# Opening of an FFT filter and max-of-two MoE kernel: another order of loads, preparations and the first stage of batch 1

## Chip, cores and metric

The kernel runs on one core of one Trainium2 chip. The metric is device time in microseconds (us), the median of the runs of one program. Engines are named as the profile names them: PE (TensorE, matmul; PEld its weight loads), DVE (VectorE), ACT (ScalarE), POOL (GpSimd) and SP (SyncE, which only issues DMAs here).

## What is computed

```python
X = np.fft.rfft(x, axis=1)                       # x: 8 x 3072 x 256
Y = X * (filt_r + 1j * filt_i)[None]             # filters: 1537 x 256
y = np.fft.irfft(Y, n=3072, axis=1)
h1, h2 = y @ w1, y @ w2                          # w1, w2: 256 x 1024
out = np.maximum(h1, h2) @ w_out                 # w_out: 1024 x 256
```

The kernel uses max(h1, h2) = relu(h1 - h2) + h2. With Wd = w1 - w2 and M = w2 @ w_out the last two lines become relu(y Wd) w_out + y M.

## The kernel before

**Stages.** Each of the 8 batches passes a first transform over 96 points (f1 for batch 1 and s1 for later ones; s1t for batch 0), a regrouping of its result into bt, six visits, each of which makes a second transform (s2, PSUM tile px), a product with the filter F (pq) and the way back (s3, tile pz), a regrouping into zr, a last transform (s4, PSUM tile py, result y), and the MoE part in tiles of 384 tokens, eight tiles per batch.

For batch 0 the two regroupings are transposes on PE: t1 fills bt[0], s3t and t2 fill zT and zr[0]. For batch 1 and later they go through DRAM: f1 or s1 write `ad` (SP), f1_read or s1_read read `ad` into bt (SP); s3 writes `zd`, z_read reads it into zr.

**The MoE loop.** A tile tt has eight steps, one for each block j of 128 hidden columns; step 8*i + j is counted within a batch. A step issues, in this order: moe_h(tt, j), two matmuls with Wd into a PSUM tile ph and a relu copy to gt on DVE or ACT; a visit of the next batch if `mid` has one for this step; three or four of the 30 matmuls of moe_o for the tile before (po: two with M and eight with Wo for each of three blocks c of 128 tokens); then what `todo` holds for the step; and at j = 4 s4 of the next tile (j = 6 at the batch's last tile). So tile 0's output matmuls run in steps 8 to 15, beside tile 1's moe_h.

**What sets the order.** Every engine runs its instructions in program order; the schedule is written out by hand. `plan(b, step, fn, ...)` puts a call in `todo` at a step, plan_f1 places f1 (c = 1 to 15) and f1_read of batch 1, plan_f2 places the visits, the loads of x of the batch after (load_xf on SP, fold on POOL), z_read and s1_read. An instruction waits by semaphore for what it reads and for the buffer that it writes. PSUM tiles of the pool `ps` come from a ring of six, those of `pso` (po) from a ring of two.

**Queues.** POOL issues load_x (x of batches 0 and 1, one call loads the xb tile of two c; x(1,0), x(1,2), x(1,4), x(1,6) below are load_x(1, c, 2)), load_f (the filters), load_wo (w_out as bf16 into Wo), the output, and it computes products of the opening, prep_wd and fold. SP issues load_w (w1, w2 into WS, the tile that w1f and w2f are views of), double_f of the second filter part, the ad, bt, zd and zr transfers and load_xf.

**The opening.** load_f(0) loads filter columns w = 0 to 7, load_f(1) w = 8 to 11, each into partitions 0 to 31 of two groups g, for real and imaginary part ri. double_f(h, g, ri, engine) copies such a quarter to the 32 partitions beside it: for h = 0 on DVE (L130), for h = 1 by DMA on SP (L132). fix_f sets one row. Visits 0 to 3 of batch 0 read the h = 0 quarters, visits 4 and 5 the h = 1 quarters. products(v) computes one half of a visit's product on DVE and, for v in 0, 2, 3, 4, the other on POOL; v = 5 shares it.

**Preparations.** cast_w2(h, c) casts a quarter of w2 to bf16 (DVE, L285), prep_t(jp) transposes four blocks of it into w2T (PE L299, ACT L300), prep_m multiplies w2T and Wo to M (16 matmuls, L306, and a copy on ACT, L308). prep_wd(h) computes half of Wd on POOL (L292). table_ct makes CT, which s1 of batch 2 reads.

The calls of the opening that the change moves, and the schedule of tile 0, stand at L580 to L640 and L677 to L688.

Of the kernel before, what the change touches and what calls it, by code (L numbers as in the profile page):

```python
# [8 lines left out]
FP32 = mybir.dt.float32  # L9
# [17 lines left out]
def kernel(  # L27
# [55 lines left out]
    def load_x(b, c, n):  # L83
        for k in range(c, c + n):
            xb[b, k] = x_tile(b, k)[0:NP]
        src = x[b].rearrange("(p m) d -> p m d", m=NM)
        m0 = 4 * (c % 2)
        G.dma_start(out=xb[b][0:NP, m0:m0 + 4 * n], in_=src[:, 4 * c:4 * c + 4 * n, :])  # L88
# [37 lines left out]
    def double_f(h, g, ri, engine):  # L126
        w0, w1 = WP[h]
        o_, i_ = F[64 * g + 32:64 * g + 64, ri, w0:w1], F[64 * g:64 * g + 32, ri, w0:w1]
        if engine is V:
            V.tensor_copy(o_, i_)  # L130
        else:
            nc.sync.dma_start(out=o_, in_=i_)  # L132
# [6 lines left out]
    def fix_f():  # L139
        V.tensor_copy(F[32:33, 0, 0, 0], FN[32:33])  # L140
# [28 lines left out]
    load_f(0)  # L169
    load_f(1)  # L170
    load_fn()
    load_x(1, 0, 2)

    def table_c():
        p96 = init.tile([128, 1], FP32)
# [111 lines left out]
    def load_wo():  # L287
        G.dma_start(out=Wo, in_=moe_w_out.rearrange("(c p) j -> p c j", p=128))

    def prep_wd(h, engine):  # L290
        js = slice(512 * h, 512 * h + 512)
        engine.tensor_tensor(Wd[:, :, js], w1f[:, :, js], w2f[:, :, js], OP.subtract)  # L292

    def prep_t(jp):
# [162 lines left out]
    def out_block(tt, c):  # L457
# [2 lines left out]
        E = G if tt < 8 * B - 2 else nc.sync  # L460
        E.dma_start(out=dst, in_=ot[tt // 2][:, 3 * (tt % 2) + c])  # L461

    def moe_o(tt, k0, k1):
        y_, g_ = yt[tt], gt[tt]
        for k in range(k0, k1):
            c, e = divmod(k, 10)
            n = (e + 2) % 10 if tt == 0 else e
            q = 3 * tt + c
            blk = slice(128 * c, 128 * c + 128)
            if e == 0 and (q % 2 == 0 or q == 24 * B - 1):  # L470
                po[0] = pso.tile([128, 2, D], FP32, tag="po", name="po")
            p_ = po[0][:, q % 2]
            if n < 2:
                TE.matmul(p_, y_[:, n, blk], M[:, n], start=(e == 0), stop=(e == 9))  # L474
            else:
                TE.matmul(p_, g_[:, n - 2, blk], Wo[:, n - 2], start=(e == 0), stop=(e == 9))  # L476
            if e == 9 and q >= 24 * B - 2:
                e = q % 6
                if q % 2 == 0:
                    S.activation(ot[tt // 2][:, e], p_, AF.Copy)  # L480
                else:
                    V.tensor_copy(ot[tt // 2][:, e], p_)
                out_block(tt, c)
            elif e == 9 and q % 2 == 1:
                if q % 6 == 1:
                    ot[tt // 2] = opool.tile([128, 6, D], FP32, tag="ot", name="ot")
                e = q % 6
                V.tensor_copy(ot[tt // 2][:, e - 1:e + 1], po[0])  # L488
                for qq in (q - 1, q):
                    out_block(qq // 3, qq % 3)  # L490

# [64 lines left out]
    def spin(n):  # L556
        for _ in range(n):
            pd = ps.tile([128, 512], FP32, tag="ps", name="pd")
            TE.matmul(pd, W1[:, 0:128], W1, start=True, stop=True)  # L559
# [12 lines left out]
    for c in range(8):  # L572
# [5 lines left out]
        if c < 7:  # L578
            spin(2)
    bt[0] = bpool.tile([128, NU, D], BF16, tag="bt", name="bt")  # L580
    for n in range(6):
        t1(n, S if n % 2 else V)
    put_v(0, 0, table_v(0, 0))
    for g in range(2):
        for ri in range(2):
            double_f(0, g, ri, V)
            if g == 0 and ri == 0:
                fix_f()
    xs = {}

    def stage_x(v):
# [6 lines left out]
    def products(v):  # L598
        pool = pq0 if v > 2 else pqpool
        pq = [product(V, v, 0, pxs[v][0], pool)]  # L600
        if v == 5:
            pq.append(shared_product(v, 1, pxs[v][1], xs[v], pool))
        else:
            pq.append(product(G, v, 1, xs[v], pool) if v in POOLED else product(V, v, 1, pxs[v][1], pool))
        return pq
# [11 lines left out]
    put_v(1, 1, table_v(1, 1))  # L617
    for v in (1, 0, 2):
        pqs[v] = products(v)
    s3t(1, pqs[1])  # L620
    pxs[4] = s2(0, 4)
    stage_x(4)
# [7 lines left out]
        pqs[v] = products(v)  # L630
    for v in (4, 5):
        s3t(v, pqs[v])
    for c in (2, 4):
        load_x(1, c, 2)
    prep_wd(0, G)
    load_wo()
    load_x(1, 6, 2)
    prep_wd(1, G)
    table_ct()
    setup.close()  # L640
    apool = ctx.enter_context(tc.tile_pool(name="apool", bufs=3))
# [4 lines left out]
    f1(1, 0, S)  # L646
    spin(1)
    t2(0, (V, S))
    spin(2)
    s4(0)  # L650
    spin(2)


# [2 lines left out]
    def plan(b, step, fn, *a):  # L656
        todo.setdefault((b + step // 64, step % 64), []).append((fn, a))
# [17 lines left out]
            plan(b, steps[-1] + (6 if b else 11), s1_read, b + 2)  # L675

    plan(0, 2, t2, 1, (V,))  # L677
    for h in range(2):
        for c in range(2):
            plan(0, 3 + 2 * h + c, cast_w2, h, c)  # L680
    plan(0, 5, prep_t, 0)
    plan(0, 7, prep_t, 1)
    plan(0, 8, prep_m)
    for c in range(2, 8):
        plan(0, 8 * (c - 2) + 8, t2, c, (V,))
    plan_f1(0, 1, (0, 1, 1, 3, 4, 4, 5, 6, 6, 7, 8, 10, 11, 11, 12), 13)
    plan_f2(0, (24, 28, 31, 35, 38, 42, 46), ((0,), (1,), (2,), (3,), (4,), (5,), (6, 7)),
            (6, 10, 14, 18, 21, 25, 29, 33), (14, 18, 21, 25, 28, 32, 36, 40))  # L688
    for b in range(1, B - 1):
        plan_f2(b, (7, 14, 18, 24, 31, 38, 42) if b > 1 else (14, 18, 24, 30, 34, 39, 42), ((0, 1), (2,), (3,), (4,), (5,), (6,), (7,)),  # L690
# [49 lines left out]
```

## Time and profile before

| | us |
|---|---|
| runs of the kernel (three) | 503.27, 505.98, 503.62; median 503.62 |
| profiled execution, whole | 503.8 |
| profiled execution, span from first to last instruction | 502.0 |
| PE busy within the span | 488.4 (97%) |
| DVE busy | 331.9 (66%) |
| ACT busy | 308.3 (61%) |
| POOL busy | 257.5 (51%) |
| mean granted TensorE clock | 0.992 of full |

The profile gives one execution. "Busy" counts instructions, not DMA issues' waiting; a matmul's busy time includes its way through the array, so that matmuls overlap: two of ph last 0.49 us together but take 0.33 us of the chain. The page cuts the span into 40 slices of 12.55 us; a digit is the busy share in tenths. In a timeline row stand the start, the time from the start to the end of the group, the engine, the line in the kernel, the operation, the output and input tiles, how many, and in brackets how long the engine was idle before and what ended that. A row of DMA issues gives the bytes of one and the time from issue to landing.

### The profile page before, as it was taken

How to read it: one execution, taken by the hardware profiler on the slowest of the kernel's cores; microseconds unless marked ns; L12 is line 12 of the kernel's file. 1: busy time of each engine (PE TensorE's matmuls, PEld its weight loads, DVE VectorE, ACT ScalarE, POOL GpSimd, SP SyncE). 2: the span in 40 equal slices, each digit the busy share in tenths (PEclk: the TensorE clock that was granted, in tenths of full speed). 3: DMA queues.
4: the chain of work that ended last, by engine and by line, in shares of the span. 5: the costliest groups of instructions: out<-in, count | busy, mean ns of one | idle time of the engine just before them, and what ended most of it. 6: DMA issues, size and time to landing. Idle time of an engine off the chain costs nothing.

```text
span 502.0 us, 13079 instructions
## 1 busy us (share of the span) xinstructions
PE 488.4 (97%) x5299; PEld 362.1 (72%) x5303; DVE 331.9 (66%) x518; ACT 308.3 (61%) x629; POOL 257.5 (51%) x338
## 2 busy tenths in 40 slices
PE   8688999999999999999999999999999999999997
PEld 3455777777777777777777777777777777777775
DVE  7876688457865777457765687557765687555553
ACT  6776478647774676557764586647774465544442
POOL 7893569547463864645654855537632221222220
PEclk9989999999999999999999999999999999999999
DMA  7999789995799667986779558896769235411112
GB/s 125 150 252 217 230 229 290 306 274 171 212 268 260 175 204 234 250 229 189 198 244 275 187 177 245 235 239 197 197 181 255 78 111 153 168 65 64 64 64 84
DMA packets 77966, 97.20 MB, mean 194 GB/s; under 512 B 8017, under 2 KB 54354, under 8 KB 77842
## 3 DMA queue, kind: packets, MB, share of 16 engines
q1 hardware_dynamic: 64642, 66.73, 49.6%
q0 software_dynamic: 13264, 29.64, 20.3%
q8 instruction: 41, 0.67, 0.6%
q14 instruction: 19, 0.16, 0.1%
HBM read 53.87 MB, written 47.19 MB: 201 GB/s over the span
## 4 chain that ended last, share of the span: by engine, by line
PE 90%; DMA 5%; POOL 2%; issue 1%; ACT 1%; DVE 0%; SPq 0%; POOLq 0%; DVEq 0%
PE po L476 34%; PE ph L448 33%; PE po L474 8%; PE pz L399 5%; PE py L428 4%; PE pa L349 2%; DMA F<-in_filt_r_dram 2%; PE px L376 2%; DMA Wo<-in_moe_w_out_dram 2%; POOL xb L88 1%; DMA F<-F 1%; PE pr L549 1%; POOL pq L382 0%; PE pt L528 0%; PE pm__1132 L306 0%
## 5 line engine op out<-in xcount | busy, mean ns | idle before, releaser
L476 PE MATMUL po<-Wo,gt 128*128 128x256 bf16 x1536 | 261.0, 273 | 0.2 <-DMA Wo<-in_moe_w_out_dram 0.2
L452 ACT ACTIVATE gt<-ph 128x384 bf16<-128x384 f32 x321 | 157.0, 496 | 147.9 <-PE ph L448 147.3
L461 POOL DMA_DIRECT2D out_dram<-ot x186 | 102.6, 555 | 187.1 <-DVE ot L488 184.4
L476 PEld LDWEIGHTS <-gt 128*128 128x128 bf16 x1536 | 146.6, 98 | 66.1 <-issue 10.3
L450 DVE TENSOR_SCALAR gt<-ph 128x384 bf16<-128x384 f32 x191 | 104.9, 552 | 63.1 <-PE ph L448 59.9
L382 DVE TENSOR_TENSOR pq<-px,F 128x1024 bf16<-128x1024 f32 x91 | 107.0, 1219 | 24.2 <-PE px L376 22.6
L448 PEld LDWEIGHTS <-Wd 128*128 128x128 bf16 x1024 | 96.5, 98 | 12.9 <-POOL Wd L292 1.4
L103 POOL TENSOR_TENSOR xb<-XF 128x512 bf16<-128x512 f32 x48 | 61.2, 1276 | 41.3 <-DMA XF<-in_x_dram 21.2
L488 DVE COPY ot<-po 128x512 f32<-128x512 f32 x95 | 65.1, 685 | 25.3 <-PE po L476 25.0
L104 POOL TENSOR_TENSOR xb<-XF 128x512 bf16<-128x512 f32 x48 | 61.0, 1271 | 0.0
L403 ACT ACTIVATE zt<-pz 128x512 bf16<-128x512 f32 x84 | 45.6, 595 | 11.5 <-PE pz L399 8.4
L353 ACT ACTIVATE at<-pa 128x512 bf16<-128x512 f32 x96 | 51.8, 610 | 1.2 <-PE pa L349 0.8
L428 PE MATMUL py<-G,zr 96*128 96x96 bf16 x512 | 32.7, 206 | 0.2
L428 PEld LDWEIGHTS <-zr 96*128 96x128 bf16 x512 | 29.0, 97 | 2.5 <-DVE zr L552 0.4
L399 PE MATMUL pz<-pq,VP 64*64 64x256 bf16 x336 | 21.9, 281 | 0.0
L376 PE MATMUL px<-bt,U 64*64 64x256 bf16 x384 | 19.8, 278 | 1.2 <-ACT VQ L273 0.7
L399 PE MATMUL pz<-pq,VQ 64*64 64x256 bf16 x336 | 20.9, 269 | 0.0
L349 PE MATMUL pa<-xb,CT 64*64 64x512 bf16 x192 | 19.5, 383 | 0.0
L399 PEld LDWEIGHTS <-VP 64*64 64x64 bf16 x336 | 9.7, 105 | 13.3 <-issue 13.3
L376 PEld LDWEIGHTS <-U 64*64 64x64 bf16 x384 | 10.4, 109 | 3.9 <-issue 3.3
L559 PE MATMUL pd<-W 128*128 128x512 bf16 x30 | 10.5, 462 | 1.7 <-DVE zero L145 1.5
L552 DVE COPY zr<-pr 96x1024 bf16<-96x1024 bf16 (+1 forms) x8 | 5.2, 649 | 8.0 <-PE pr L549 8.0
(429 smaller groups left out, 609.7 us busy)
## 6 DMA issues: line engine op xcount, KB each, us to landing
out_dram<-ot POOLq DMA_DIRECT2D x186, 128.0 KB, 3.3
XF<-in_x_dram SPq DMA_DIRECT2D x96, 192.0 KB, 4.6
ad<-at SPq DMA_DIRECT2D x56, 192.0 KB, 3.3
bt<-ad SPq DMA_DIRECT2D x14, 768.0 KB, 9.1
zd<-zt SPq DMA_DIRECT2D x42, 256.0 KB, 2.7
zr<-zd SPq DMA_DIRECT2D x56, 192.0 KB, 4.8
WS<-in_moe_w_dram SPq DMA_DIRECT2D x4, 512.0 KB, 5.1
xb<-in_x_dram POOLq DMA_DIRECT2D x8, 192.0 KB, 5.8
```

What stands on the lines that cost most here:

```text
L103: G.tensor_tensor(t_[:, 0], f[:, 0], f[:, 1], OP.add)
L104: G.tensor_tensor(t_[:, 1], f[:, 0], f[:, 1], OP.subtract)
L353: S.activation(at[:, m0:m0 + 2], pa[g], AF.Copy)
L382: E.tensor_tensor(pq, px.rearrange("p (o i) d -> p o i d", o=1).to_broadcast([128, 2, 2, D]), F[:, :, 2 * v:2 * v + 2, s], OP.mult)
L399: TE.matmul(pz[g][64 * s:64 * s + 64, i], tab[64 * g:64 * g + 64, 2 * v + i, s], pq[s][64 * g:64 * g + 64, q, i], start=(q == 0), stop=(q ...
L428: TE.matmul(py[:, m], zr[b][:, 4 * i + m, 128 * dc:128 * dc + 128], G1, start=True, stop=True)
L448: TE.matmul(ph, Wd[:, dc, 128 * j:128 * j + 128], y_[:, dc], start=(dc == 0), stop=(dc == 1))
L450: V.tensor_scalar(gt[tt][:, j], ph, 0.0, None, OP.max)
L452: S.activation(gt[tt][:, j], ph, AF.Relu)
L461: E.dma_start(out=dst, in_=ot[tt // 2][:, 3 * (tt % 2) + c])
L476: TE.matmul(p_, g_[:, n - 2, blk], Wo[:, n - 2], start=(e == 0), stop=(e == 9))
L488: V.tensor_copy(ot[tt // 2][:, e - 1:e + 1], po[0])
```

## The change

- x(1,0) is no longer issued by POOL ahead of the products, but between products(0) and products(2).
- Of the four h = 0 filter copies on DVE, the first (g = 0, real) stands ahead of the bt copies of t1. fix_f and the other three stay behind put_v(0, 0, ...), fix_f now ahead of the three.
- prep_wd computes a quarter (256 columns) at a time. POOL's order behind the products was x(1,2), x(1,4), Wd half 0, Wo, x(1,6), Wd half 1; it is x(1,2), Wo, Wd quarters 0 and 1, x(1,4), quarters 2 and 3, x(1,6).
- The two casts of w2's first half stand in the opening, on both sides of s4(0); those of the second half come in steps 3 and 4 (were 5 and 6). prep_t(0) comes in step 3 (was 5), prep_m in step 9 (was 8).
- FIRST gives the order of tile 0's output matmuls: the Wo matmuls of blocks c = 0 and 2, then their M matmuls, then block c = 1. Since blocks 0 and 2 lie in two po tiles, po is kept by q // 2 % 2.
- f1 of batch 1, c = 1 to 15, comes in steps 0, 1, 1, 4, 5, 5, 6, 8, 9, ... 15 instead of 0, 1, 1, 3, 4, 4, 5, 6, 6, 7, 8, 10, 11, 11, 12; f1_read in step 16 (was 13). The visits of batch 1, its z_read and s1_read of batch 2 come two steps later. load_xf and fold of batch 2 stay where they were: load_xf(2, 2), in step 14, is thus now ahead of the last ad write and of f1_read on SP.

```diff
-    load_x(1, 0, 2)
...
     def prep_wd(h, engine):
-        js = slice(512 * h, 512 * h + 512)
+        js = slice(256 * h, 256 * h + 256)
...
+    FIRST = ([(c, e) for c in (0, 2) for e in range(8)] + [(c, e) for c in (0, 2) for e in (8, 9)]
+             + [(1, e) for e in range(10)])
...
-            c, e = divmod(k, 10)
-            n = (e + 2) % 10 if tt == 0 else e
+            c, e = divmod(k, 10) if tt else FIRST[k]
+            n = e if tt else (e + 2) % 10
...
-                po[0] = pso.tile([128, 2, D], FP32, tag="po", name="po")
-            p_ = po[0][:, q % 2]
+                po[q // 2 % 2] = pso.tile([128, 2, D], FP32, tag="po", name="po")
+            p_ = po[q // 2 % 2][:, q % 2]
...
-                V.tensor_copy(ot[tt // 2][:, e - 1:e + 1], po[0])
+                V.tensor_copy(ot[tt // 2][:, e - 1:e + 1], po[q // 2 % 2])
...
+    double_f(0, 0, 0, V)
     for n in range(6):
         t1(n, S if n % 2 else V)
     put_v(0, 0, table_v(0, 0))
-    for g in range(2):
-        for ri in range(2):
-            double_f(0, g, ri, V)
-            if g == 0 and ri == 0:
-                fix_f()
+    fix_f()
+    double_f(0, 0, 1, V)
+    for ri in range(2):
+        double_f(0, 1, ri, V)
...
     for v in (1, 0, 2):
         pqs[v] = products(v)
+        if v == 0:
+            load_x(1, 0, 2)
...
-    for c in (2, 4):
-        load_x(1, c, 2)
+    load_x(1, 2, 2)
+    load_wo()
     prep_wd(0, G)
-    load_wo()
+    prep_wd(1, G)
+    load_x(1, 4, 2)
+    prep_wd(2, G)
+    prep_wd(3, G)
     load_x(1, 6, 2)
-    prep_wd(1, G)
...
     t2(0, (V, S))
+    cast_w2(0, 0)
     spin(2)
     s4(0)
+    cast_w2(0, 1)
...
-    for h in range(2):
-        for c in range(2):
-            plan(0, 3 + 2 * h + c, cast_w2, h, c)
-    plan(0, 5, prep_t, 0)
+    for c in range(2):
+        plan(0, 3 + c, cast_w2, 1, c)
+    plan(0, 3, prep_t, 0)
     plan(0, 7, prep_t, 1)
-    plan(0, 8, prep_m)
+    plan(0, 9, prep_m)
...
-    plan_f1(0, 1, (0, 1, 1, 3, 4, 4, 5, 6, 6, 7, 8, 10, 11, 11, 12), 13)
-    plan_f2(0, (24, 28, 31, 35, 38, 42, 46), ((0,), (1,), (2,), (3,), (4,), (5,), (6, 7)),
+    plan_f1(0, 1, (0, 1, 1, 4, 5, 5, 6, 8, 9, 10, 11, 12, 13, 14, 15), 16)
+    plan_f2(0, (26, 30, 33, 37, 40, 44, 48), ((0,), (1,), (2,), (3,), (4,), (5,), (6, 7)),
             (6, 10, 14, 18, 21, 25, 29, 33), (14, 18, 21, 25, 28, 32, 36, 40))
```

## The prediction

> **What bounds the kernel now.** I read the page's slices first. PE is full from the fourth slice on, at the full granted clock; only the first 50 us of the 502.0 us span hold idle time of PE.
>
> ```profile
> PE   8688999999999999999999999999999999999997
> PEclk9989999999999999999999999999999999999999
> ```
>
> So the end moves only by PE work added or removed, and by PE idle time in the first 50 us or newly made later. The change adds no matmul. Next the PE timeline from 34 us shows where PE idles while tile 0 runs: for the second half of Wd, for a cast of w2, and shortly for Wo.
>
> ```profile
> 37.48 0.62 PE L448 MATMUL ph<-y__984,Wd 128*128 128x384 bf16 x2 [0.19 <-ACT y__984 L432]
> ...
> 41.07 0.50 PE L448 MATMUL ph<-y__984,Wd 128*128 128x384 bf16 x2 [0.67 <-POOL Wd L292]
> ...
> 45.35 0.56 PE L299 MATMUL pt<-I,w2b 128*128 128x128 bf16 x7 [0.70 <-DVE w2b L285]
> ...
> 46.64 0.60 PE L476 MATMUL po<-Wo,gt 128*128 128x256 bf16 x4 [0.18 <-DMA Wo<-in_moe_w_out_dram]
> ```
>
> From first ph (37.48) to first po (46.64) are 9.16 us. Their work at the chain's prices (ph pair 0.33, f1 0.22, eight transposes 0.45, py 0.34): nine ph pairs, ten f1, t2(1), s4(1), two prep_t = 6.86. So 2.3 us are idle. From 46.64 on the chain of waits is PE behind PE, apart from small gaps: 455.36 us to the end.
>
> The POOL timeline shows the order of its loads; the third row is Wo, the fourth x(1,6).
>
> ```profile
> 33.83 1.06 POOL L88 DMA_DIRECT2D xb<-in_x_dram  x2
> 34.90 2.36 POOL L292 TENSOR_TENSOR Wd<-WS 128x1024 bf16<-128x1024 f32 x1
> 37.19 0.93 POOL L288 DMA_DIRECT2D Wo<-in_moe_w_out_dram  x1
> 38.12 0.52 POOL L88 DMA_DIRECT2D xb<-in_x_dram  x1
> 38.65 2.36 POOL L292 TENSOR_TENSOR Wd<-WS 128x1024 bf16<-128x1024 f32 x1
> ```
>
> The DMA view, asked for single issues, gives landings (last column, us after the issue): Wo 9.4, so 46.6; x(1,6), queued behind Wo, 10.9, so 49.0; x(1,2), issued 33.83 with no Wo ahead, 5.3, so 39.1.
>
> ```profile
> Wo<-in_moe_w_out_dram POOLq DMA_DIRECT2D x1, 512.0 KB, 9.4
> xb<-in_x_dram POOLq DMA_DIRECT2D x1, 384.0 KB, 10.9
> xb<-in_x_dram POOLq DMA_DIRECT2D x1, 384.0 KB, 5.3
> ```
>
> POOL's transfers are thus served one after another: Wo held x(1,6) until 2.4 us after its own landing. Last, batch 1's first visit. SP's timeline and the waits of 60 to 64 us: bt is read at 56.88, lands 5.8 us later at 62.7, and px wants it at 62.97. There is no slack.
>
> ```profile
> 56.88 1.22 SPq L338 DMA_DIRECT2D bt<-ad  x2
> PEld L376 <- DMA bt<-ad: 0.3, 1, 0.3
> ```
>
> **Opening.** DVE now copies bt at 15.64, 16.54 and 17.43, then the four filter quarters from 18.15 to 23.32 (1.22 each, fix_f 0.28). The first quarter's last load (8 KB, issued 8.66, 7.0 to land) arrives at 15.7, so the moved copy runs 15.8 to 17.0, bt follows back to back to 19.05, and the last quarter ends at 22.9: 0.4 us earlier. bt 0.9 us later is hidden: px of visit 0 waits for ACT's last bt (18.94) anyway.
>
> But products 4 and 5 wait for the second filter half: its last load is issued by POOL at 22.28, its doubling on SP at 26.45 lands 4.0 later at 30.45, and DVE and POOL start product 4 at 30.60 and 30.63. While a filter copy runs on DVE, POOL's issues take 1.25, 1.49, 1.24 and 1.17 us, else 0.48 to 0.58; each ends just behind a copy. So the first copy, moved to 15.8, holds POOL's issue of 15.66 until 17.0, 0.8 us; POOL later escapes one copy. The last load is issued 0 to 0.5 us earlier.
>
> [...]
>
> x(1,0) is issued behind POOL's first product: about 25.7 instead of 23.43. Product 0 starts at 23.5 instead of 24.02, and the 0.52 of issue goes behind it, so product 3 still ends at about 30.4: nothing won on POOL. Its data now meets the last doubling, not the third. The third, which met it, took 5.4; the second, which didn't, 3.2; the last 4.0. Opening: from -0.3 (earlier issue) to +1.4 (4.0 becoming 5.4). I take 0: the earlier issue against a partial collision, since the doubling goes out beside x(1,0), not after it.
>
> **Tile 0.** POOL ends product 5 at 33.89. Then x(1,2) 0.53, Wo 0.93, two quarters of Wd 1.18 each (half of 2.36), x(1,4) 0.53, two quarters, x(1,6): Wo issued 34.4 instead of 37.19; Wd quarters ready at 36.5, 37.7, 39.4, 40.6; x(1,4) issued 37.7 instead of 34.36; x(1,6) 40.6 instead of 38.12. If each cast of w2 (0.41) blocks POOL as the filter copies did, the last quarter comes at 42.2, just when ph of j=6 wants it; I take nothing, at most 0.4.
>
> Two casts go into DVE's idle gaps before y (0.97) and the first at (0.63): free; without those gaps 0.82. Three f1 leave steps 0 to 7. DVE, which now runs unbroken from 38.36 to 45.89, then needs from 41.09 only cast, gt, cast, y, at, 0.41+0.54+0.41+0.54+0.68, until 43.7. That frees the PSUM room (six in the ring) of tile 1's first ph, so PE is ready for po at 44.1.
>
> Wo: it lands 5.5 to 6.2 us behind the x ahead of it (x(1,4) landed at 40.4 to 41.1, Wo at 46.6). With only x(1,2) ahead (39.1) that is 44.6 to 45.3; bounds 44.1 (it hides) and 46.6 (no gain). I take 44.7. The gain is 46.64 - 44.7 = 1.94, less the three moved f1, 3 x 0.22 = 0.65: 1.3.
>
> FIRST and prep_m one step later cost nothing. M's copy (0.60) now ends well before matmul 16 of tile 0 at step 12; without that cover it's 0.6. The second po buffer is held to step 16, and next wanted at step 18, 2 us later, against 0.68 for the copy.
>
> **f1 8.** In step 8 PE runs po (0.44), t2(2) (0.45) and then f1 8, the first reader of x(1,4): wanted at 45.6. x(1,4) is behind Wo as x(1,6) was, and lands 2.4 after it: 47.1. PE is in order, so the next ph, all po and prep_m wait behind f1 8: 1.5 us. Bounds: 0, if it lands like x(1,2) (37.7 + 5.3), and 2.4. I take 1.5, since the row with Wo ahead is the one that fits. x(1,6) then lands about 49.5, f1 12 wants it after 52: hidden.
>
> **Batch 1's bt.** Now from f1 15 (ends 53.30) to px PE has 9.54 us of work: steps 13 to 24, t2, two s4. In the changed order f1 15 stands in step 15 and px in step 26: eleven ph pairs 3.6, 37 po 4.0, two t2 0.9, one s4 0.34 = 8.9, that is 0.66 less. Ahead of f1 15's copy DVE now has tile 0's ot copy, which waits for po's last matmul: at is ready 1.35 us behind f1 15 instead of 0.9. On SP, load_xf(2,2)'s four transfers, formerly behind the reads of bt, go out just ahead of the last ad write; the ad write that stood right behind such a group took 3.1 to land, the next 2.6. Sum: 0.66 + 0.47 + 0.5 = 1.6, less 0.3 for the reads that no longer share with those transfers: 1.3 us of PE idle. Bounds 0 and 2.3. Visits and z_read are two steps later throughout: zr of batch 1 is issued by 96.4, lands 4.8 later at 101.2, and the first py on it runs at 106.87; the 5.7 us shrink to about 4. Hidden.
>
> **Sum.** 502.0 + 0 - 1.3 + 1.5 + 1.3 = 503.5, that is +1.5. The profiled execution took 503.8 with 1.8 outside the span; the median of the runs shown is 503.62. On the median: 505.1 us. About 0.5% (2.5 us) is what a measurement of this kernel tells from no change.
>
> **Rivals.**
> - *Only one of the two arrivals is late.* For it: x(1,2)'s 5.3 would bring x(1,4) at 43; bt's read could be quicker with its rings clear. Against: 10.9 behind Wo. No f1 wait gives -1.9 + 1.3 = 503.0, no px wait 503.8; 503.4 in the middle.
> - *Everything hides; Wo in time at 44.1:* -2.54 + 0.65 = -1.9, 501.7. For it: 1.5 of the 2.3 idle us hang on Wd and the casts, which do come sooner. Against: bt's lack of slack.
> - *x(1,0) pushes the last doubling back* to 5.4 us, decided at product 4 near 31.8. All behind it, Wo too, comes 1.4 later: 506.5. For it: the third doubling's 5.4. Against: the last one's 4.0 already overlaps x(1,0).
> - *A stall drops PE's clock; the side opposite to a gain or no change.* The granted clock fell to 0.50 near 22.8 us, after 3.4 us in which PE was busy 1.37, and came back at 29.3. If PE's wait for x(1,4) or bt does this, 6.5 us of saturated PE at half clock cost 3.2: 508.3. It decides when such a wait leaves PE about 40% busy over 3.4 us, so from 2 us up. Against: around 41 to 46 us PE idled 0.7 twice and the clock stayed 1.00.
>
> [...]
>
> **Chances.** Forecast 0.40; one arrival only 0.22; everything hides 0.12; doubling late 0.13; clock 0.13. The forecast's own range is 503.8 to 506.6. 80%: 501.6, near the bottom of what hides, to 507.4, leaving out most of the clock's case. Faster by over 0.5% (below 501.1) needs all hidden and a shorter opening: 0.07. Slower (above 506.1): most of the two last rivals and a tail of the forecast, 0.24. Within: 0.69.
>
> **What would show it.** Right: POOL's filter issue near 15.7 takes about 1.3 us; Wo lands 44 to 45.5; PE idles over 1 us at f1 8 with the x load as releaser; PE idles over 1 us at the first px near 63 to 65 with bt<-ad as releaser. Wrong: PE unbroken from po on, or x(1,4) landing before Wo; then the time is near 502. A half clock past 45 us, or product 4 after 31.5, gives the slower rivals.

## The result and the profile after

| | before | after |
|---|---|---|
| median (6 runs each, same chip) | 503.52 | 508.25 |
| lowest to highest | 502.9 to 505.98 | 506.94 to 509.2 |
| profiled execution, whole | 503.8 | 508.3 |
| its span | 502.0 | 506.5 |

The ratio after / before is 1.0083, 95% interval 1.0059 to 1.0108: the changed kernel is slower by 4.2 us by this ratio (the medians lie 4.7 apart), outside the predicted range. Line numbers of the changed kernel are one less (L447 is ph, L375 px) or three more (L479 is po with Wo) than those of the kernel before.

The page's slices of the changed kernel, PE's busy tenths and the granted clock (a slice is 12.66 us):

```profile
PE   8689989999999999999999999999999999999997
PEclk9989989999999999999999999999999999999999
```

The sixth digit, 63.3 to 76.0 us, is new in both rows: an 8 where the kernel before had 9. The fourth of PE, where tile 0 runs, rose from 8 to 9. Where the time went is seen best from the start of each MoE tile, the first ph matmul with its y in PE's timeline of either kernel (my table, us):

| tile starts | 0 | 1 | 2 | 3 | 4 | 7 | 63 |
|---|---|---|---|---|---|---|---|
| before | 37.48 | 45.97 | 55.82 | 62.48 | 72.52 | 96.95 | 489.07 |
| after | 39.46 | 45.73 | 55.96 | 62.62 | 74.76 | 101.44 | 493.55 |
| later by | 1.98 | -0.24 | 0.14 | 0.14 | 2.24 | 4.49 | 4.48 |

So 2.0 us are lost in the opening, 1.84 won up to tile 3 (the three moved f1 already paid in tile 1), 4.35 lost in tiles 3 to 6, which hold the visits, and nothing is won or lost behind tile 7. First the opening, in POOL's timeline of the changed kernel:

```profile
16.09 1.49 POOL L120 DMA_DIRECT2D F<-in_filt_i_dram  x1 [0.30 <-DMA F<-in_filt_r_dram]
...
19.57 1.48 POOL L117 DMA_DIRECT2D F<-in_filt_r_dram  x1
21.04 1.28 POOL L120 DMA_DIRECT2D F<-in_filt_r_dram  x1
22.32 1.13 POOL L117 DMA_DIRECT2D F<-in_filt_i_dram  x1
23.44 0.53 POOL L120 DMA_DIRECT2D F<-in_filt_i_dram  x1
24.04 2.13 POOL L381 TENSOR_TENSOR pq<-xs,F 128x1024 bf16<-128x1024 f32 x1
26.11 0.57 POOL L88 DMA_DIRECT2D xb<-in_x_dram  x1
...
32.63 2.12 POOL L381 TENSOR_TENSOR pq<-xs,F 128x1024 bf16<-128x1024 f32 x1 [1.71 <-DMA F<-F]
```

Four issues take over 1.1 us, one for each filter copy on DVE, as before; the moved copy holds the issue of 16.09. The last filter load is issued at 23.44 (before 22.28). x(1,0) goes out at 26.11. Product 4 starts at 32.63 (before 30.63), behind the last doubling, which was issued at 27.71 (before 26.45) and took 4.8 us (before 4.0). In the DMA view this doubling before, after, and x(1,0) after:

```profile
F<-F SPq DMA_DIRECT2D x1, 128.0 KB, 4.0
F<-F SPq DMA_DIRECT2D x1, 128.0 KB, 4.8
xb<-in_x_dram POOLq DMA_DIRECT2D x1, 384.0 KB, 4.8
```

Now PE's timeline, with tile 0's first ph, the first po and the first px of batch 1:

```profile
39.46 0.62 PE L447 MATMUL ph<-y__987,Wd 128*128 128x384 bf16 x2
46.05 0.60 PE L479 MATMUL po<-Wo,gt 128*128 128x256 bf16 x4
67.04 0.41 PE L375 MATMUL px<-bt,U 64*64 64x256 bf16 x8 [1.96 <-DMA bt<-ad]
```

From first ph to first po are 6.6 us (before 9.16) without a bracketed wait. The one wait is that of px. The chain of waits, in order of time, says what it hangs on:

```profile
55.61 0.56 DVE gt L449
56.17 0.60 DVE ot L491
56.77 0.60 DVE at L326
...
57.43 4.84 DMA ad<-at
62.27 0.02 issue
62.29 4.71 DMA bt<-ad
67.00 0.04 issue
67.04 0.41 PE px L375 x8
```

The last ad write takes 4.84 us. In the kernel before the read of bt followed its issue by 2.6, as SP's timeline there shows:

```profile
54.25 0.32 SPq L332 DMA_DIRECT2D ad<-at  x1
56.88 1.22 SPq L338 DMA_DIRECT2D bt<-ad  x2
```

In the chain above, tile 0's ot copy stands ahead of the at copy. Last, the windows of one us behind that wait; the columns are the busy time of PE, PEld, DVE, ACT and POOL, then PEclk, DMA share and GB/s:

```profile
66.00:67.00 1.00, 0.00 (x0) 0.00 (x0) 0.00 (x0) 0.00 (x0) 0.99 (x2) 1.00 1.15 347
67.00:68.00 1.00, 0.96 (x15) 0.58 (x16) 0.50 (x1) 0.28 (x1) 0.00 (x0) 0.87 1.15 348
68.00:69.00 1.00, 1.00 (x6) 0.54 (x5) 1.00 (x2) 0.80 (x2) 0.00 (x0) 0.50 1.21 393
69.00:70.00 1.00, 1.00 (x6) 0.64 (x5) 0.86 (x1) 0.49 (x1) 0.00 (x0) 0.50 1.02 305
70.00:71.00 1.00, 1.00 (x6) 0.64 (x5) 0.00 (x0) 0.49 (x1) 0.00 (x0) 0.50 1.01 313
71.00:72.00 1.00, 1.00 (x14) 0.79 (x13) 0.32 (x1) 0.49 (x1) 0.68 (x1) 0.93 1.08 260
```

The clock is at 0.50 for three windows and at 0.87 and 0.93 beside them: 0.13 + 3 x 0.50 + 0.07 = 1.7 us of PE work lost in 3.4 us at half clock, where a ph pair takes 0.64 us of the chain instead of 0.33. With the wait of 2.0 that is 3.7 of the 4.35.

### The profile page after: what moved, and what is told of

Read it like the earlier page. It is cut to its first block, busy times and chain, and to the rows that moved or that the text cites. A ratio compares the mean times of both kernels' runs of the same rounds, so it can differ in the third digit from the quotient of the medians.

```text
span 506.5 us, 13083 instructions
## 1 busy us (share of the span) xinstructions
PE 492.0 (97%) x5303; PEld 362.9 (72%) x5303; DVE 333.1 (66%) x518; ACT 309.0 (61%) x629; POOL 258.4 (51%) x340
## 4 chain that ended last, share of the span: by engine, by line
PE 88%; DMA 6%; POOL 3%; DVE 1%; ACT 1%; issue 0%; POOLq 0%; SPq 0%
PE po L479 33%; PE ph L447 32%; PE po L477 8%; PE pz L398 5%; PE py L427 4%; PE pa L348 3%; PE px L375 2%; DMA F<-in_filt_r_dram 2%; DMA ad<-at 1%; DMA F<-F 1%; DMA bt<-ad 1%; DMA F<-in_filt_i_dram 1%; POOL xb L88 1%; POOL F L117 1%; POOL F L120 1%; DMA zd<-zt 1%
## 5 line engine op out<-in xcount | busy, mean ns | idle before, releaser
L479 PE MATMUL po<-Wo,gt 128*128 128x256 bf16 x1536 | 261.9, 274 | 0.0
L479 PEld LDWEIGHTS <-gt 128*128 128x128 bf16 x1536 | 147.2, 98 | 66.3 <-issue 10.4
L381 DVE TENSOR_TENSOR pq<-px,F 128x1024 bf16<-128x1024 f32 x91 | 107.1, 1220 | 27.6 <-PE px L375 23.9
L447 PEld LDWEIGHTS <-Wd 128*128 128x128 bf16 x1024 | 96.8, 98 | 12.3 <-issue 0.7
L375 PE MATMUL px<-bt,U 64*64 64x256 bf16 x384 | 19.9, 280 | 3.4 <-DMA bt<-ad 2.0
L375 PEld LDWEIGHTS <-U 64*64 64x64 bf16 x384 | 10.3, 109 | 6.3 <-issue 3.6
L348 PEld LDWEIGHTS <-CT 64*64 64x64 bf16 x192 | 8.8, 105 | 2.7 <-ACT gt L451 1.2
```

What stands on the lines that cost most here:

```text
L381: E.tensor_tensor(pq, px.rearrange("p (o i) d -> p o i d", o=1).to_broadcast([128, 2, 2, D]), F[:, :, 2 * v:2 * v + 2, s], OP.mult)
L447: TE.matmul(ph, Wd[:, dc, 128 * j:128 * j + 128], y_[:, dc], start=(dc == 0), stop=(dc == 1))
```

## The experiments

All are made from the changed kernel unless another is named; each ratio is against the kernel before on the same chip. In this table "ph" is tile 0's start, "doubling" the last one's time to landing, "ad" the time from the last ad write's issue to the read of bt, "px" PE's wait there, all in the one profiled execution.

| run | what it is | median, us (n) | ratio, 95% | ph | doubling | ad | px |
|---|---|---|---|---|---|---|---|
| after | | 508.25 (6) | 1.0083, 1.0059 to 1.0108 | 39.46 | 4.8 | 4.8 | 1.96 |
| e1 | filter copy back | 507.48 (6) | 1.0078, 1.0049 to 1.0107 | 39.68 | 2.2 | 4.6 | 1.63 |
| e2 | x(1,0) back | 505.9 (9) | 1.0047, 1.0029 to 1.0065 | 38.03 | 4.3 | 4.6 | 1.50 |
| e3 | both back | 505.83 (7) | 1.0044, 1.0019 to 1.007 | 37.64 | 5.4 | 4.5 | 1.46 |
| e4 | visits 2 later | 506.68 (6) | 1.0051, 1.0033 to 1.0069 | 38.13 | 4.9 | 4.7 | 0 |
| e5 | load_xf(2,2) behind bt | 508.67 (12) | 1.0079, 1.005 to 1.0108 | 39.90 | 5.8 | 3.9 | 0.92 |
| e6 | e3, casts back | 505.69 (12) | 1.0023, 1.0001 to 1.0045 | 37.95 | 5.1 | 4.3 | 1.35 |
| e7 | e6, x(1,0) behind product 2 | 507.81 (12) | 1.0068, 1.0041 to 1.0095 | 38.10 | 4.6 | 4.5 | 1.35 |
| e8 | e6, load_xf(2,2) behind bt | 506.15 (12) | 1.0034, 1.0013 to 1.0055 | 37.90 | 4.4 | 4.1 | 0.97 |
| e9 | e6, FIRST undone | 507.96 (6) | 1.0074, 1.0054 to 1.0093 | 38.24 | 4.5 | 5.5 | 2.41 |
| e10 | e9, f1 denser | 505.36 (12) | 1.0014, 1.0 to 1.0028 | 37.56 | 4.0 | 3.7 | 0 |
| e11 | e6, visits 2 sooner | 509.07 (6) | 1.0091, 1.0069 to 1.0113 | 38.62 | 5.5 | 4.9 | 3.69 |
| e12 | e6, visits 2 later | 504.77 (12) | 1.0012, 0.9996 to 1.0028 | 38.57 | 3.2 | 4.0 | 0 |
| e13 | e8 and e9 together | 504.91 (12) | 1.0021, 1.0003 to 1.0038 | 37.85 | 4.2 | 2.1 | 0 |
| e14 | e16, casts on ACT | 504.06 (12) | 1.0007, 0.9983 to 1.0031 | 37.46 | 4.4 | 4.5 | 0 |
| e15 | before, x(1,0) moved alone | 504.79 (12) | 1.0016, 1.0002 to 1.0029 | 39.71 | 5.7 | 2.3 | 0 |
| e16 | e3, visits 2 later | 504.56 (12) | 1.0011, 0.9993 to 1.0028 | 37.54 | 3.1 | 4.3 | 0 |
| e17 | e13, e3's casts on ACT | 504.47 (12) | 1.0023, 1.0003 to 1.0042 | 37.39 | 3.7 | 2.0 | 0 |
| e18 | e14, s1_read of batch 2 in step 57 | 503.51 (12) | 0.9986, 0.9974 to 0.9998 | 37.90 | 3.2 | 4.5 | 0 |

### The opening: e1, e2, e3, e7, e15

e1 puts the first filter copy back behind the bt copies, e2 puts x(1,0) back ahead of the products, e3 does both.

```diff
-    double_f(0, 0, 0, V)
     for n in range(6):
         t1(n, S if n % 2 else V)
     put_v(0, 0, table_v(0, 0))
+    double_f(0, 0, 0, V)
```

```diff
     load_fn()
+    load_x(1, 0, 2)
...
-        if v == 0:
-            load_x(1, 0, 2)
```

> The changed kernel with the first filter copy put back behind the bt copies; x(1,0) stays behind product 0. Theory (the copy, wherever it runs, costs POOL's issuing one blocked issue, and at 16.2 us it comes before all of the second filter half): POOL's last filter load starts near 22.3 instead of 23.44, the last doubling goes out near 26.4 and, still beside x(1,0), lands 4.8 later at 31.2; product 4 at 31.3 instead of 32.6, the time about 1.3 us below the changed kernel, 507. Rival (x(1,0) alone makes the doubling late): the last load moves, product 4 stays after 32, the time stays at 508.

> The changed kernel with x(1,0) put back ahead of POOL's products; the first filter copy stays ahead of bt. Theory of the copy: the last filter load still starts near 23.4, the doubling goes out at 27.5 and lands 4.0 later, product 4 at 31.5 to 31.8, 0.8 to 1.1 us below the changed kernel, 507.3. Rival (x(1,0) alone): product 4 returns to 30.6, 2 us below, 506.2.

> Both put back, the rest of the change kept. If the two together are the whole loss of the opening: product 4 at 30.6 +- 0.3, first ph at 37.5, the time 2.0 us below the changed kernel, 506.2; the wait for bt at the first px and the half clock behind it stay. If something else in the opening counts (the loads' own scatter), product 4 stays above 31.3.

Putting the copy back changes the ratio by 0.0005 and 0.0003, far inside the intervals; putting x(1,0) back takes 0.0036 off, 1.8 us. e3's profile meets its expectation for the opening (product 4 at 30.80, first ph at 37.64); the wait for bt stays, and the half clock behind it does not come. The profiled e1 was the second highest of its six executions (510.38, highest 510.54), for a reason that comes below under the casts. e7 asks again from the other side, out of e6 (x(1,0) behind product 2), and e15 moves x(1,0) alone in the kernel before:

> e6_casts_back with x(1,0) issued behind POOL's product 2, at about 28. Theory (the last doubling is slow, 4 to 5.5 us, only beside x(1,0)): it lands 2.2 to 3 us after its issue near 26, as in e1_copy_back, and product 4 then waits for POOL alone, near 30.4: equal to e6_casts_back or 0.3 below. If x(1,0) alone made the loss and any later place costs as much, 1.5 to 2 above e6_casts_back.

> The kernel before with one edit: x(1,0) issued by POOL behind product 0 instead of ahead of the products. Theory 'x(1,0) costs by itself': inside the change it cost 1.8 (the changed kernel against e2) and 2.1 us (e7 against e6, there behind product 2), so here the median is 1.2 to 2.3 above the kernel before, ratio 1.0025 to 1.0045; in the profile the last doubling takes over 4.5 us or product 4 starts past 31.5, or f1 1 waits for xb. Rival 'it costs only together with the rest (Wo sooner behind it in POOL's queue)': within 0.6 us of the kernel before, ratio 0.999 to 1.0012.

e7 costs 0.0045, 2.2 us, more than e6; e15 0.0016, 0.6 to 0.8 us, between its two theories. The DMA view gives the reason as far as it goes. In every kernel x(1,0) and the last doubling share some time. In the 18 kernels in which x(1,0) goes out first, the doubling takes 3.1 to 4.3 us where x(1,0) has still 1.6 to 2.6 us to fly, and 4.0 to 5.8 where it has 3.2 to 5.1.

Behind product 0 (after, e4, e5, e15) x(1,0) lands later, at 30.4 to 30.9 instead of 28.8 to 30.3, and the doubling with it: at 31.1 to 32.5, mean 31.9, where it took 4.8, 4.9, 5.8 and 5.7 us, mean 5.3. In the 14 kernels (before among them) with x(1,0) ahead of the products it lands at 29.6 to 31.0, mean 30.4, and takes 3.1 to 5.5, mean 4.2. Tile 0 starts at 39.3 on average in those four, at 37.9 in the 14.

In e1 and e7 x(1,0) goes out 1.5 and 1.3 us behind the doubling, which takes 2.2 and 4.6. e1's doubling thus landed first of all, at 28.4; its late tile 0 has another reason: POOL's product 0 waited 2.44 us for DVE's filter copies and started at 25.64 (24.04 in the changed kernel). The copy's place, though, changes nothing: the last filter load's issue ends at 23.6 on average in the four kernels with the copy ahead, at 23.3 in the 16 others.

A late product 4 can cost once more. In the profiles of e5 and e15 PE, waiting for it, idled about 2.2 of the 3.4 us before 35.4 and 35.0, and the granted clock fell to 0.50 for the next 3.4 us. From product 4 to tile 0 these two need 7.6 us, the changed kernel and the kernel before 6.8 to 6.9. e7's profiled execution (505.98) shows no such fall and none of the 2.2 us of its median, but the mean granted clock, which is on record for each execution, does. A stretch of 3.4 us at half clock lowers it by 0.003 (3.4 x 0.5 / 503). Seven of e7's twelve executions have a mean of 0.990 or less and take 509.56 in the median; the other five, with 0.992 or 0.993, take 505.98, near e6's 505.69. Over all six kernels with x(1,0) later, 27 of 54 executions have 0.990 or less; over the other kernels of the table but e11, 26 of 130. Where the clock fell in an execution that was not profiled is not known, and such a fall need not cost much (e15: 505.14 against 504.77). Why x(1,0) costs three times as much inside the change as alone is not explained.

### The casts: e6, e16, e14

e6 is e3 with the casts of w2 and prep_t(0) in their old steps:

```diff
-    cast_w2(0, 0)
     spin(2)
     s4(0)
-    cast_w2(0, 1)
...
-    for c in range(2):
-        plan(0, 3 + c, cast_w2, 1, c)
-    plan(0, 3, prep_t, 0)
+    for h in range(2):
+        for c in range(2):
+            plan(0, 3 + 2 * h + c, cast_w2, h, c)
+    plan(0, 5, prep_t, 0)
```

> Both parts of the opening put back as in e3_both_back, and the casts of w2 and prep_t(0) too (steps 3 to 6, step 5). Theory (a cast that stands ahead of y on DVE can meet POOL's Wd and wait 1 to 3 us for it, in some executions): the scatter of e3_both_back, 503.9 to 509.2, shrinks to about 2 us, the median falls by 0.5 to 1.5, to 504.5 to 505.3, and no ph waits for y. Rival (the casts cost nothing where they were, the scatter comes from the loads): the same median or, with 0.8 us of casts back among tile 0's copies, 0.5 above; the same scatter.

e6's median is that of e3 (505.69, 505.83; by the ratios e6 is 1.1 us lower, inside the intervals), although e3's first po came 1.7 us sooner (44.24, 45.94): in e3 something takes back in the median what the profile wins. e16 (e3 with visits in 28, 32, 35, 39, 42, 46, 50) and e14 (e16 with the casts as activations on ACT) ask what.

> The kernel of e3 (first filter copy and x(1,0) as before the change, casts in the opening as in the change; 505.83 us, px wait 1.46) with the visits of batch 1 two steps later (28, 32, 35, 39, 42, 46, 50). Theory 'the terms add': the wait of 1.46 goes, 504.2 to 504.7, ratio 1.0005 to 1.0025. Rival 'the casts on DVE scatter by what POOL's Wd holds them, and that is most of e3's loss': it stays above 505, with casts of over 0.8 us or a wait for y in the profile where it falls on such an execution.

> The kernel of e16 with the four casts of w2 on ACT instead of DVE. In e3's profile ACT has gaps of 0.35 and 0.71 us where the first two stand, so each of about 0.6 holds ACT's y or gt by 0.1 to 0.3 us. Theory 'POOL's Wd holds DVE's casts, and ACT's not': no cast over 0.8 us, first po at 44 to 45 as in e3 (44.2; before 46.6), and the median 0.5 to 1.5 below e16: 503.0 to 504.2, ratio 0.997 to 1.0; it may be the fastest of all. Rival 'ACT is as tight as DVE here': ACT's relu and at copies come late, PE waits for gt or ph room, the median is at or above that of e16.

e16's median is what "the terms add" expected. Its profile fell on the highest execution of twelve (508.63) and shows the rival at work. DVE's timeline of e16 around the first cast, and POOL's of the same time:

```profile
35.83 0.42 DVE L556 COPY zr<-pr 96x512 bf16<-96x512 bf16 x1 [0.58 <-PE pr L553]
36.17 4.97 DVE L285 CAST w2b<-WS 128x512 bf16<-128x512 f32 x1
41.07 0.54 DVE L434 TENSOR_SCALAR y__987<-py 128x384 bf16<-128x384 f32 x1
```

```profile
35.36 2.52 POOL L292 TENSOR_TENSOR Wd<-WS 128x512 bf16<-128x512 f32 x2
37.79 0.56 POOL L88 DMA_DIRECT2D xb<-in_x_dram  x1
38.36 2.49 POOL L292 TENSOR_TENSOR Wd<-WS 128x512 bf16<-128x512 f32 x2
```

The cast, 0.41 us when alone, takes 4.97: it is held from 36.2 until POOL's fourth Wd quarter ends near 40.8, and y behind it holds PE, in the view of waits (total, times, longest):

```profile
PE ph L448 <- DVE y__987 L434: 3.8, 1, 3.8
```

The same cast took 0.8 in the changed kernel, e2 and e3, 2.42 in e4 and 3.42 in e1, and e5's second cast took 1.90; how many quarters a cast is caught behind varies. On ACT (e14) all four take 0.62 to 0.63, and first po stands at 44.43. e14's median is 0.5 below e16's, at the edge of its expectation and inside the intervals. So the mechanism is shown; its share of the medians is not. Three of e14's twelve lie over 507, and these are the three with a mean granted clock of 0.990 or less; the other nine have a median of 503.51.

### The late bt: e4, e12, e11, e5, e8, e9, e10, e13

e4 (on the changed kernel) and e12 (on e6) put the visits two steps later, e11 (on e6) two sooner:

```diff
-    plan_f2(0, (26, 30, 33, 37, 40, 44, 48), ((0,), (1,), (2,), (3,), (4,), (5,), (6, 7)),
+    plan_f2(0, (28, 32, 35, 39, 42, 46, 50), ((0,), (1,), (2,), (3,), (4,), (5,), (6, 7)),
```

> The changed kernel with the visits of batch 1 two steps later still (28, 32, 35, 39, 42, 46, 50). Theory (bt is read too late for the visit): PE's wait of 2.1 us at the first px falls to 0.6 or less, the granted clock stays 1.00 behind it, which saves 1.5 to 2.1 and another 1.6 us: 504.5 to 505.2. Rival (the visits' later place makes new waits, at zr of batch 1 or by crowding DVE): the wait goes but the time falls by less than 1.5 us.

> The kernel of e6 with the visits of batch 1 two steps later still (28, 32, 35, 39, 42, 46, 50). Theory 'the px wait is a term of the sum by its own length': the wait of 1.35 goes, no clock drop, nothing else is late, and the median is 1.0 to 1.6 below e6, 504.1 to 504.7, level with the kernel before within 0.2%. Rival 'the visits two steps later make zr late': PE waits for zr at the first py of batch 1 or the next batch's bt, 0.5 us or more, and the median is at most 0.5 below e6.

> The kernel of e6 with the visits of batch 1 in their steps before the change (24, 28, 31, 35, 38, 42, 46), bt read as late as in e6: the first px is wanted two steps, about 1.9 us, sooner and PE waits some 3.2 us there instead of 1.35. Theory 'a long enough wait halves the granted clock': in the changed kernel it fell to 0.50 for 3.2 us behind a wait of 2.0; here it falls to 0.50 for 3 us or more in the profiled execution, and the median rises by more than the added wait: 1.9 + 1.6 = 3.5, to 508.8 to 509.8. Rival 'the clock follows something else than this wait': the clock stays at 1.00 or the median rises by only 1.5 to 2.1, to 507.2 to 507.8.

Without the wait e4 is 1.6 below the changed kernel (ratios 1.0083, 1.0051), between its theory and its rival, and not the 3.7 of wait and clock in the changed kernel's profile. The clock falls in other places too: four of e4's six executions still have a mean of 0.990 or less, as four of the changed kernel's six have, and take 506.59 to 508.37; the two others take 505.26 and 505.64. e12 is 0.6 (by ratios) to 0.9 (by medians) below e6, against a wait of 1.35, again between theory and rival. With a longer wait e11 rises by 3.4 (1.0091, 1.0023), 2.3 of it wait (3.69 less 1.35). Its windows show the rest:

```profile
64.00:66.00 2.00, 0.00 (x0) 0.00 (x0) 0.00 (x0) 0.17 (x1) 2.00 (x2) 1.00 0.89 263
66.00:68.00 2.00, 0.72 (x12) 0.37 (x12) 0.04 (x1) 0.00 (x0) 1.48 (x3) 0.78 1.15 348
68.00:70.00 2.00, 2.00 (x17) 1.53 (x14) 2.00 (x2) 1.08 (x2) 0.00 (x0) 0.50 1.14 322
70.00:72.00 2.00, 2.00 (x16) 1.41 (x15) 1.38 (x3) 0.47 (x1) 0.41 (x1) 0.87 1.04 287
```

The clock is halved again for 3.4 us, here at the end of a wait of 3.7; all six executions of e11 have a mean of 0.990 or less. Next, why the last ad write is slow. e5 (on the changed kernel) and e8 (on e6) take the XF group from ahead of it, e9 (on e6) takes the outputs of tile 0 from beside it, e13 does both, e10 is e9 with f1 8 to 15 in steps 8 to 13 and f1_read in 14:

```diff
-            (6, 10, 14, 18, 21, 25, 29, 33), (14, 18, 21, 25, 28, 32, 36, 40))
+            (6, 10, 17, 18, 21, 25, 29, 33), (14, 18, 21, 25, 28, 32, 36, 40))
```

```diff
-            c, e = divmod(k, 10) if tt else FIRST[k]
-            n = e if tt else (e + 2) % 10
+            c, e = divmod(k, 10)
+            n = (e + 2) % 10 if tt == 0 else e
...
-    plan(0, 9, prep_m)
+    plan(0, 8, prep_m)
```

> The changed kernel with load_xf(2, 2) in step 17, behind the reads of bt. Theory (its four transfers hold up the last ad write): the write lands in 2.1 to 2.6 us instead of 4.8, the reads, now followed by those transfers as in the kernel before, take up to 5.8 instead of 4.7, so PE's wait at the first px falls from 2.0 to 0.3 to 1.0 and the half clock behind it does not come: 1 to 3 us below the changed kernel. Rival (the write is late for another reason, the output's transfers or its late start behind the ot copy): it still takes over 4, the wait stays near 2.

> e6_casts_back with load_xf(2, 2) behind the reads of bt as well: what is left of the change is W_out sooner, Wd in quarters, FIRST, prep_m and the later f1 and visits. If the wait for bt is what is left of the loss: PE waits under 0.7 at the first px, and the time is 502.0 to 503.0, 1 to 2 below the kernel before. Rival (the later f1 and visits lose elsewhere what tile 0 gains): 503.5 to 504.5.

> The kernel of e6 (opening and casts as before the change; 505.69 us, its last ad write read back 4.3 us after its issue, first px waiting 1.35 us for bt), with tile 0's output matmuls in their old order and prep_m in step 8 again. Theory 'the output held it': FIRST finishes blocks 0 and 1 of tile 0 only in step 15, so that DVE's copy of ot stands just ahead of the last at copy and POOL's first two output writes (128 KB each) run beside the last ad write. Then here the outputs of these blocks leave by 56 us or earlier, the last ad write takes 2.1 to 3.2 us as in the kernel before (2.6), bt is read 1 us or more sooner, the first px waits under 0.6 us, and the median is 0.8 to 1.5 us below e6: 504.2 to 504.9. Rival 'the write is slow for its own place': it is slow because XF transfers of 4 x 64 to 192 KB go out just ahead of it, or by its mere size; then it takes about 4 us again, px waits 1.2 to 1.5 and the median stays within 0.4 of 505.7.

> The kernel of e8 (opening and casts as before the change, load_xf(2, 2) only behind the read of bt) with tile 0's output matmuls and prep_m in their old order. Theory 'two neighbours, either is enough': the last ad write is slow by the XF group ahead of it or by the outputs beside it; with both away it is read back within 3.3 us of its issue (e8 4.1, e9 5.5, the kernel before 2.6), bt is read by 60.6, the first px waits under 0.4. Rival 'the write is slow by itself': it takes 3.9 us or more again, px waits 0.9 or more. For the median the write hardly counts here, since zr came late in e8 too: theory 505.2 to 505.9, rival 506 to 506.6.

> As e9, and f1 of batch 1 closer together: c = 8 to 15 in steps 8, 9, 9, 10, 11, 11, 12, 13 instead of 8 to 15, f1_read in step 14 instead of 16; visits stay in step 26. Theory 'bt is read too late, and nothing else is wrong behind tile 0': f1 15 comes two steps (about 1.8 us) earlier, px waits for nothing, and the median falls by the wait that e9 leaves (0 to 1.4), to 503.8 to 504.6, level with the kernel before. Rival 'the early part is worth something only when f1 is spread': with eight f1 in six steps DVE and the ring of ps delay ph and po, PE gaps of over 0.3 us appear between 46 and 58 us, and the median is not below that of e9.

One neighbour away is not enough, and neither e5 nor e8 gains what its theory expected: e5's wait falls from 1.96 to 0.92, but its median stays at that of the changed kernel; e8's falls from 1.35 to 0.97 and its median is no lower than e6's. SP's timeline of e9, with the XF group ahead and the outputs sooner (POOL issues the first two at 54.96 and 55.55, over 2 us ahead of the write):

```profile
55.69 0.42 SPq L93 DMA_DIRECT2D XF<-in_x_dram  x1
56.16 0.44 SPq L97 DMA_DIRECT2D XF<-in_x_dram  x1
56.65 0.42 SPq L93 DMA_DIRECT2D XF<-in_x_dram  x1
57.12 0.45 SPq L97 DMA_DIRECT2D XF<-in_x_dram  x1
57.67 0.36 SPq L332 DMA_DIRECT2D ad<-at  x1
63.20 1.16 SPq L338 DMA_DIRECT2D bt<-ad  x2
```

In e8 it is the other way round: no XF ahead, outputs issued at 56.82, the ad write at 57.2, bt read at 61.27. With both away, SP's timeline of e13 (the last of the three writes is issued at 56.7):

```profile
53.05 3.98 SPq L332 DMA_DIRECT2D ad<-at  x3
58.77 1.18 SPq L338 DMA_DIRECT2D bt<-ad  x2
```

2.1 us, and px waits for nothing; e17 confirms it with 2.0. So either neighbour is enough to keep the write about 2 us longer: in the table "ad" is 2.0 to 2.3 with neither of them (e13, e17, and e15, which has the old order), 3.7 to 5.5 with one or both. e9's theory fell; its rival named the right neighbour but expected a wait of 1.2 to 1.5 and e6's median, and the wait was 2.41 and the median 2.3 to 2.6 over e6: not explained. e13's theory held in the profile, and its median is below what both expected. e10's px has no wait, but PE waits 1.2 us for zr; by ratios it is 3.0 us below e9 and 0.7 above the kernel before.

### Versions that mend it: e17, e18

e17 mends everything found: the old opening, casts on ACT, FIRST undone, load_xf(2,2) behind bt. e18 is e14 with one read placed by hand:

```diff
-            plan(b, steps[-1] + (6 if b else 11), s1_read, b + 2)
+            plan(b, steps[-1] + (6 if b else 7), s1_read, b + 2)
```

> The changed kernel with all three causes mended: first filter copy and x(1,0) as before the change, the four casts of w2 on ACT, tile 0's output matmuls in the old order and load_xf(2, 2) behind the read of bt. Kept are Wo sooner, Wd in quarters, the casts sooner, f1 and the visits later. Theory 'these three are the whole loss': first po at 44.4 to 45 as in e14 (before 46.6), last ad write read back within 3.3 us, px wait under 0.5, no half clock, and the median is that of the kernel before less 1.75 (46.64 - 44.24 - 0.65) and plus up to 1.2 for what was never accounted for (f1 8's wait of 0.4, some 0.5 of small waits): 502.4 to 503.7, ratio 0.9965 to 0.999. Rival 'the later f1 and visits cost by themselves what Wo gains': zr or the next batch's bt comes late (e14's profile had a wait of 2.8 for it), and the ratio is 1.0 or more.

> The kernel of e14 (casts on ACT, visits in 28, 32, ...) with the read of batch 2's bt in step 57, where it stood before the change, instead of 61. In the kernel before it is issued 17.1 us ahead of its first px (97.47, px 114.61), in e14 12.7 (100.64, px 113.33), in e17 14.0; all its ad writes are issued by 94.8 in e14. Theory 'the read that moved along with the visits makes the tail': issued at 97 to 98, at least 15 us ahead, no wait for bt of batch 2, no execution above 505.5, and the median 0.3 to 0.9 below e14's 504.06: ratio 0.996 to 0.9995. Rival 'the tail comes from elsewhere (the opening, x loads)': two or more of twelve stay above 506.5, median within 0.3 of 504.1.

e17's profile has no PE wait over 0.3 us behind tile 0's start and a span of 501.7, yet the number of its rival came: the median is 504.47, without the late zr or bt that the rival named. Of the 1.95 us that it is ahead at tile 1, 0.68 go with the f1 in tile 1 and 0.9 in tiles 3 to 6, the visits, where no wait over 0.2 shows; e13 loses the same 0.9 there, e12 0.4. Counted from one matmul's start to the next, 0.63 of the 0.9 lies behind the 32 pa matmuls of batch 2's first stage (3.07 us, before 2.44) and 0.24 behind those of pr. Three of e17's twelve executions, those over 507, have a mean granted clock of 0.989; the other nine have a median of 503.84. e18 is the one kernel under the one before: 0.14%, interval 0.02 to 0.26%. The reason for e18 was e14's profile, an execution of 508.26 in which PE waited for bt of batch 2:

```profile
113.33 0.29 PE L376 MATMUL px<-bt,U 64*64 64x256 bf16 x1
116.42 0.64 PE L376 MATMUL px<-bt,U 64*64 64x256 bf16 x7 [2.80 <-DMA bt<-ad]
```

In e4's profile, with visits in the same steps, the same wait was 0.8. Three of e14's twelve lie over 507, none of e18's over 505.16. But e18's read was still issued at 102.40 and not at 97 to 98. The last ad write had been issued at 96.93 and landed at 101.2, and SP had first to issue z_read's four transfers (99.63 to 101.33, after 2.2 us of waiting for zd) and two of XF. The read stood 13.5 us ahead of its px, expected at least 15, against 12.7 in e14. e18's median, 503.51, is that of e14's nine executions without a low clock: e18 is e14 without its tail, on another chip. That the step made the tail go is thus suggested by the counts, not shown. The profile of e18, its highest execution, has another wait of the prediction: f1 8 for x(1,4).

```profile
47.79 0.42 PE L324 MATMUL pa<-xb,C 96*96 96x512 bf16 x1 [1.35 <-DMA xb<-in_x_dram]
```

## Why the prediction was wrong

**PE bounds the kernel; only what delays PE early counts.** Right: from tile 7 on the two kernels keep 4.48 to 4.49 us apart to the end.

**Opening, forecast 0, measured +2.0.** This is the step that failed first. I gave the third doubling's 5.4 as the upper bound for a doubling beside x(1,0), and took 4.0 because "the doubling goes out beside x(1,0), not after it". The runs show the upper bound: 5.3 on average with x(1,0) behind product 0, a landing 1.5 later (31.9 against 30.4) and a tile 0 that starts 1.4 later. The reading under the 4.0 was wrong too: the second doubling was said not to have met x(1,0), but it was issued at 21.61 and took 3.2, so that it met it from 23.43 on. A doubling's time went with how long x(1,0) had still to fly: in the 18 kernels 3.1 to 4.3 us where that was 1.6 to 2.6, 4.0 to 5.8 where it was 3.2 to 5.1. In the changed kernel's profile the doubling took 4.8, 0.8 more than before; the rest of the 2.0 is its issue, 1.26 later, of which no run shows the reason (it lies between 25.0 and 27.6 in the 14 kernels). "POOL later escapes one copy" was wrong for this execution and doesn't matter on average (23.6 against 23.3). The rival that x(1,0) pushes the last doubling back, at 1.4 us, was the truth of this part, though this profile shows only 0.8 of it as a longer doubling.

**Tile 0, forecast -1.3, measured -1.84.** Right, a little small. The term mis-sized is Wo's transfer: forecast 10.3 us (34.4 to 44.7), measured 7.1 (36.37 to 43.5). It landed 4.0 us behind the first ph instead of 7.2, and po did not wait.

**The casts, forecast free.** Wrong in a way that the trace of before could not show, where they stood behind Wd's first half. I asked how DVE's cast would hold POOL (0.4), not how POOL's Wd would hold the cast: 0.4 in the changed kernel's profile, 4.6 in e16's. In e16 the cast started at 36.17, during the first two Wd quarters, and ended at 41.14, behind the fourth (40.85), so that POOL's next quarters passed the waiting cast too; in e1 it took 3.42. What decides which of the two engines holds the other, no run here shows.

**f1 8, forecast 1.5, measured 0.** The size was wrong for this execution: x(1,4), issued 39.96, landed 7.0 later, and f1 8 ran just then, since the opening was 2 us late. In the other profiles that reached po as early or earlier than 46.05 with the casts in their new places it waited 0.4 (e2, e3), 1.35 (e18) and nothing (e14, e17). So 1.5 is the size of the worst of five. That the late opening hid a wait here is likely, since x(1,4) landed just as f1 8 was wanted, but not shown. The rival with only one late arrival was also added up wrongly: without the wait at f1 8 the forecast's terms give -1.3 + 1.3 = 0, 503.6; the -1.9 in its -1.9 + 1.3 belongs to the case that Wo comes at 44.1.

**bt, forecast 1.3, measured 2.0.** The mechanism was right; the term mis-sized is the ad write, 3.1 forecast (2.6 + 0.5), 4.8 measured. I priced the XF group ahead of it and not the outputs, which FIRST lets POOL issue at 57.06, beside the write of 57.43; e13 shows that both have to go. How the outputs hold the write is open: in e8, where nothing on SP's queue but outputs on POOL's stood ahead of it, it took 4.1.

**The clock, a rival at 3.2 us, measured 1.7.** It came, on top of the forecast and not in its place, after a wait of the very length that I named ("from 2 us up"). Behind tile 0's start it fell with waits of 2.0 (after), 2.25 (e1, for y behind a held cast), 2.8 (e14), 3.7 (e11) and 3.8 (e16), and not with 2.4 (e9) or 1.35 to 1.6 (e1, e2, e3, e6, e7). The changes themselves bring order into this: in all 20 profiles they lie whole multiples of 3.41 us apart (in the changed kernel at 23.36, 30.19, 67.74 and 71.15). Counted in such stretches, the clock fell at the end of one in which PE idled 1.96 us (after), 2.1 (e14), 2.4 (e1), 2.6 (e16) or 3.4 (e11); e9's wait lay across two, 0.8 in the first and 1.6 in the second, and the clock held. So the length of a wait alone did not decide; behind the wait of 2.0 the clock fell although PE was busy for 1.45 of the 3.41 us before. Why, no run here shows. The half clock near 22.8 in the kernel before lasted two stretches, 6.8 us and not the 6.5 that the rival was priced from.

**Visits, z_read, forecast hidden.** zr was hidden in the changed kernel (in e5, e8 and e10 it was not: 0.6 to 1.2). The stretch with the visits is nevertheless 0.65 us longer than wait and clock, 0.4 to 0.9 in e12, e13 and e17. In the changed kernel 0.62 of it lies behind the pa matmuls (3.07 us, before 2.44), without a wait that the profile shows: why is open. And I had not looked at the s1_read of batch 2, which the schedule ties to the last visit.

**Sum.** Forecast 0 - 1.3 + 1.5 + 1.3 = 1.5; measured 2.0 - 1.8 + 0 + 2.0 + 1.7 + 0.65 = 4.5. Two rivals came true together with the forecast, where the range had held each alone.

## What to carry to other kernels

A transfer moved off one crowded stretch can land in the next one (with x(1,0) moved behind product 0 the last doubling took 5.3 us on average, 4.2 without): before moving an issue, list what flies at its new time, on all queues, and price the meeting at the row that shows one. Give rivals that can be true together a joint case, since late arrivals and a halved clock added up here (2.0, 2.0 and 1.7 us), and a held cast held PE for 3.8 us in e16. Where DVE and POOL both work beside PE's critical chain, put short copies that gate the chain on ACT (a cast took 0.62 to 0.63 us there in e14, 0.41 to 4.97 on DVE in e16), and look at the time and mean clock of several executions: the one profiled may be the lucky one.

## What was not expected of the hardware

- A DVE cast of 0.41 us was held through four POOL instructions and a DMA issue between them (4.97 us, e16), during which DVE did not get its turn.
- The last ad write (192 KB) was complete 2.0 to 2.6 us after its issue with neither neighbour (before, where the outputs go out 1.3 us behind it, e13, e17), 4.1 with 256 KB of output writes beside it on POOL's queue (e8), 5.5 with 512 KB of loads just ahead of it on its own (e9).
- The half clock held for 3.4 us behind a wait of 2.0 (after, 67.74 to 71.15) and for 6.8 us behind one of 2.8 (e14, 115.7 to 122.5), so that these stalls cost 1.7 and 2.9 us more than themselves (e14: tiles 9 and 10 together took 5.7 longer than in the kernel before, 2.8 of it wait).
